# The first batch of an attention and maxout kernel: its transposes copied in two parts, and the order of its loads

## The chip, the cores and the metric

The kernel runs on one core of a Trainium2 chip. The metric is the device time of one execution in microseconds (us), as the median of several runs. The core has five engines that matter here, each working through its own instructions in order: TensorE (PE in the profile, with its weight loads shown as PEld), VectorE (DVE), ScalarE (ACT), GpSimd (POOL) and SyncE (SP). SP, ACT and POOL also issue DMA transfers; an issue stands in its engine's queue like any other instruction, and the transfer then runs on 16 DMA engines that all queues share.

## The reference

Attention over 8 batches, 12 heads, 448 tokens and 64 dimensions, with an extra term in the denominator, and behind it a feed-forward layer whose hidden value is the maximum of three products:

```python
scores = scale * np.matmul(q, k.transpose(0, 1, 3, 2))
m = np.max(scores, axis=-1, keepdims=True)
e = np.exp(scores - m)
attn = e / (np.sum(e, axis=-1, keepdims=True) + np.exp(-m) + 1e-09)
attn_out = np.matmul(attn, v)
...
x = attn_out.transpose(0, 2, 1, 3).reshape(B * S, H * D)   # 3584 x 768
h = np.maximum(np.maximum(x @ w1, x @ w2), x @ w3)
out = h @ w_out
```

All inputs and the output are float32; w1, w2, w3 and w_out are 768 x 768. With the maximum taken out, attn is exp(s) / (sum of exp(s) + 1), and this is what the kernel computes.

## The kernel before, in words

Two heads make a pair, p; a batch has NPAIR = 6 pairs, and there are NP = 48. One round `it` of the main loop computes the scores and exponentials of pair `it` and the weighted sums of pair `it - 1`.

*Loading.* `load` (L83) brings q, k or v of one or two pairs from DRAM with two DMAs each, since a tile has 128 partitions and 448 tokens are 7 chunks of 64. The upper DMA (L92) fills partitions 0 to 63 with chunks 0 to 3, the lower one (L93) partitions 64 to 127 with chunks 4 to 6. For one pair these are 128 KB and 96 KB. So a tile holds NB = 3 full chunks of 128 tokens and a last one of 64. The loads of batch 0 are issued on SP in the order in which they are written (L97 to L107), but for two halves of pair 0's that are issued on ACT. Tiles for raw data (`raw`, three sets of three pairs) are reused in turn.

*Casts.* `casts(p)` (L161) turns float32 into float16: `cast_qk` on DVE (L183 for q, L184 for k, L189 for k's last chunk, once for each head), and for pair 0 on ACT and DVE with the last chunk on POOL (L172 to L174, L189). `scale_v` (L191) multiplies v by 256 on POOL, in three instructions of line L157.

*Transposes.* `transposes(p)` (L204) makes PE transpose four chunks of q (L221) and four of k (L226) into one PSUM tile `trT`, 448 + 512 columns wide, and copies that to SBUF as `qkT`: for pair 0 in two parts (L230 on DVE, then L231 on ACT), for the others in one piece (L233 on DVE). From batch 2 on a DMA does the transposing.

*Scores.* `scores(p, c)` (L235) multiplies chunk c of k with all of q for both heads (L239), into one of two PSUM tiles; `exp_scores` (L249) takes the exponential on ACT. `scores_last` and `exp_last` (L255, L265) do the last chunk for both heads together.

*Sums.* In batch 0, `sums_main` and `sums_last` (L316, L325) give the denominators and the weighted sums apart, ACT takes the reciprocal as exp(-ln(x + 1)) (L336, L337), and DVE multiplies (L343). Later batches use L273, L285, L298, L299 and L307.

*Weights.* `load_weight` (L144) loads a matrix on POOL's queue, float32 to float16. The loop issues w1 in two halves in rounds 3 and 4 (L453), w2 in round 5, w3 in round 6 and w_out in round 8 (L455). In POOL's queue each stands behind the `scale_v` of the rounds before it.

*Feed-forward.* When a batch's attention is done, its groups are put into a queue (`batch_done`, L421): 18 groups of six matmuls (L356), six for each of w1, w2 and w3 in this order, then the output groups (L390). Rounds of the next batch take them from the queue one by one. The first three groups of batch 0, which need the first half of w1, are written out in rounds 5 and 6 (L482 to L508). The groups 3 to 5 of w1 follow in round 6, the first group of w2 is the first one of round 7.

*Filler.* `keep_busy(n)` (L345) issues n matmuls of zeros: 13 before pair 0's transposes, 3 behind them, 3 in each of the rounds 0 to 4 (L349).

The order of all instructions on each engine is the order in which the program writes them. A load on SP waits, besides for its tile, for the landing of the load eight places before it.

Of the kernel before, what the change touches and what calls it, by code (L numbers as in the profile page):

```python
# [21 lines left out]
def kernel(  # L22
# [57 lines left out]
        for i in range(NRAW)  # L80
    ]

    def load(p0, n_pairs, names="qkv", engs=(nc.sync, nc.sync)):  # L83
        b, j = divmod(p0, NPAIR)
        tiles = raw[(p0 // HB) % NRAW]
        h0 = 2 * (p0 % HB)
        for name, t, src in zip("qkv", tiles, (q, k, v)):
            if name not in names:
                continue
            rows = src[b, 2 * j : 2 * (j + n_pairs)].rearrange("h (p c) d -> p h c d", c=TP)  # L90
            hs = slice(h0, h0 + 2 * n_pairs)
            engs[0].dma_start(out=t[0:64, hs, 0 : NB + 1, :], in_=rows[:, :, 0 : NB + 1, :])  # L92
            engs[1].dma_start(out=t[64:128, hs, 0:NB, :], in_=rows[:, :, NB + 1 : TP, :])  # L93

    load(0, 1, "k", (nc.scalar, nc.sync))  # L97
    load(0, 1, "q", (nc.sync, nc.scalar))
    load(1, 1, "qk")
    load(0, 1, "v")  # L100
    load(2, 1, "qk")
    load(1, 2, "v")
    load(3, 1, "qk")
    load(4, 2, "q")
    load(3, 1, "v")
    load(4, 2, "k")
    load(4, 2, "v")  # L107

    idle = cpool.tile([128, S], MMDT, name="idle")
# [51 lines left out]
    def casts(p):  # L161
        cast_qk(p)
        scale_v(p)

    def cast_qk(p):
        qt, kt, _ = raw[(p // HB) % NRAW]
        h0 = 2 * (p % HB)
        hs = slice(h0, h0 + 2)
        k6, q6 = k16[p % NK], q16[p % NK]
        if p == 0:  # L170

            nc.scalar.copy(out=k6[:, 0:NB], in_=kt[:, hs, 0:NB].rearrange("p h c d -> p c h d"))  # L172
            for eng, cs in ((nc.scalar.copy, slice(0, 2)), (nc.vector.tensor_copy, slice(2, NB + 1))):
                eng(out=q6[:, cs], in_=qt[:, hs, cs].rearrange("p h c d -> p c h d"))  # L174
        else:
            if p >= P_DMA and (p // NPAIR) % 2:

                nc.vector.tensor_copy(
                    out=q6[:, 1 : NB + 1], in_=qt[:, hs, 0:NB].rearrange("p h c d -> p c h d")
                )  # L180
                nc.vector.tensor_copy(out=q6[64:128, 0], in_=qt[0:64, hs, NB])
            else:
                nc.vector.tensor_copy(out=q6, in_=qt[:, hs].rearrange("p h c d -> p c h d"))  # L183
            nc.vector.tensor_copy(  # L184
                out=k6[:, 0:NB], in_=kt[:, hs, 0:NB].rearrange("p h c d -> p c h d")
            )
        for hh, half in enumerate(halves):
            last = nc.gpsimd if p == 0 else nc.vector
            last.tensor_copy(out=k6[half, NB, hh], in_=kt[0:64, h0 + hh, NB])  # L189
# [14 lines left out]
    def transposes(p):  # L204
        odd = (p // NPAIR) % 2
        qkT = att_pool.tile([2 * D, 1024], MMDT, tag="qkT", bufs=3)
        qkTs[p] = qkT, 0, S
        if p >= P_DMA:
            nc.sync.dma_start_transpose(
                out=qkT.rearrange("q (c p) -> q c p", p=128),  # L210
                in_=qk16[p % NK].rearrange("p c h d -> p (c h d)"),
            )
            qkTs[p] = qkT, 64 * odd, 512
            return
        trT = ps_u.tile([128, 1024], MMDT, tag="u", name="trT")


        order = (NB, 0, 1, 2) if odd else (0, 1, 2, NB)
        n0 = 0
        for c in order:  # L220
            nc.tensor.transpose(  # L221
                out=trT[:, n0 : n0 + 128], in_=q16[p % NK][:, c], identity=ident16
            )
            n0 += SL if c == NB else 128
        for c in range(NB + 1):
            nc.tensor.transpose(  # L226
                out=trT[:, S + c * 128 : S + c * 128 + 128], in_=k16[p % NK][:, c], identity=ident16
            )
        if p == 0:
            nc.vector.tensor_copy(out=qkT[:, 0 : S + 128], in_=trT[:, 0 : S + 128])  # L230
            nc.scalar.copy(out=qkT[:, S + 128 : S + 512], in_=trT[:, S + 128 : S + 512])  # L231
        else:
            nc.vector.tensor_copy(out=qkT[:, 0 : S + 512], in_=trT[:, 0 : S + 512])  # L233

    def scores(p, c):  # L235
        qkT, q0, k0 = qkTs[p]
# [108 lines left out]
    def keep_busy(n):  # L345

        ps = ps_u.tile([128, 512], FP32, tag="u", name="busy")
        for _ in range(n):
            nc.tensor.matmul(out=ps[:, 0:S], lhsT=idle[:, 0:128], rhs=idle, start=True, stop=True)  # L349
# [81 lines left out]
            queue.pop(0)()  # L431

    LEFT = 4
    keep_busy(13)
    casts(0)
    transposes(0)
    keep_busy(3)
    for it in range(NP + 1):
        p = it if it < NP else None
        prev = it - 1 if it > 0 else None  # L440
# [14 lines left out]
            load_weight((5, 6, 8).index(it) + 1)  # L455
        if it < NPAIR:

            casts(it + 1)
            for c in range(2):
                exp_scores(p, c, scores(p, c))  # L460
            if prev is None:
                keep_busy(3)
                exp_scores(p, 2, scores(p, 2))
                transposes(1)
                exp_last(p, scores_last(p))
            else:
                den, av = (ps_av.tile([128, 512], FP32, tag="av", name=n) for n in ("den", "av"))
                sums_main(prev, den, 1)
                stp = scores(p, 2)
                sums_main(prev, av, 0)  # L470
                stl = scores_last(p)
                sums_last(prev, den, 1)
                sums_last(prev, av, 0)
                exp_scores(p, 2, stp)
                exp_last(p, stl)
                rb = reciprocals_one(den)
                transposes(it + 1)
            if it < NPAIR - 1:
                keep_busy(3)
            else:  # L480

                ups = [up_open()]  # L482
                up_part(ups[0], 0, 0, 0, range(3))
                av5 = ps_s.tile([128, 2, 512], FP32, tag="s", name="av5")
                sums_main(p, av5[:, 1], 1)
                sums_main(p, av5[:, 0], 0)
                sums_last(p, av5[:, 1], 1)
                sums_last(p, av5[:, 0], 0)
                rb5 = reciprocals_one(av5[:, 1])
            if prev is not None:  # L490
                normalize_one(prev, av, rb)
            if it == NPAIR - 1:
                normalize_one(p, av5[:, 0], rb5)
                batch_done(0)
        elif it == NPAIR:
            exp_scores(p, 0, scores(p, 0))

            up_part(ups[0], 0, 0, 0, (3,))
            ups.append(up_open())
            up_part(ups[1], 0, 0, 1, range(4))  # L500
            ups.append(up_open(ps_av, "av"))
            up_part(ups[2], 0, 0, 2, range(4))
            for dc in (4, 5):
                for fc, ps in enumerate(ups):
                    up_part(ps, 0, 0, fc, (dc,))
                    if dc == 5:
                        up_close(ps, 0, 0, fc)
            del queue[0:3]  # L508
            exp_scores(p, 1, scores(p, 1))
            group()  # L510
            casts(it + 1)
            exp_scores(p, 2, scores(p, 2))
            exp_last(p, scores_last(p))
            group()
            transposes(it + 1)
            group()
        else:
            late = it + 1 < P_DMA
            if not late:

                if it + 2 < NP:
                    cast_qk(it + 2)
                    transposes(it + 2)
                if it + 1 < NP:
                    scale_v(it + 1)
            if p is not None:
                for c in range(2):
                    exp_scores(p, c, scores(p, c))
            group()
            if late:  # L530
                casts(it + 1)
            avs = [av_main(prev, hh) for hh in range(2)]
            av_last(prev, avs)
            if p is not None:
                stp = scores(p, 2)
                stl = scores_last(p)
            rb = reciprocals(prev, avs)
            if p is not None:
                exp_scores(p, 2, stp)
                exp_last(p, stl)  # L540
            if late:
                transposes(it + 1)
            group()
            normalize(prev, 0, avs, rb)
            group()
            normalize(prev, 1, avs, rb)
            if it % NPAIR == 0:
                batch_done(prev // NPAIR)
            if it + 2 == P_DMA:
                cast_qk(it + 2)  # L550
                transposes(it + 2)
            for _ in range(n_groups - 3):
                group()
# [36 lines left out]
```

## Time and profile before

| What | Value |
|---|---|
| median of 3 runs | 368.15 us (368.03 to 368.56) |
| the profiled execution | 367.77 us |
| its span, first to last instruction | 366.0 us |
| granted TensorE clock, mean | 0.996 |
| scores of pair 0 start (PE, L239) | 7.08 us |
| scores of pair 1, 2, 3, 4, 5 start | 10.23, 14.53, 18.83, 23.48, 27.77 us |
| first matmul with w1 (PE, L356) | 31.16 us |
| DMA share of the 16 engines, 0 to 5 us and 20 to 25 us | 0.45 and 1.19 |

The profile's page begins with busy times: "busy" is time in which an engine's instructions run; issuing a DMA and waiting are not counted. In the list of groups, a row gives line, engine, operation, the tiles written and read, the shapes, the count, then the busy time in us and the mean of one in ns, and behind the second bar the idle time in front of these instructions, with what ended most of it. In the timeline a row is: start in us, duration in us, engine (with a "q" where its queue issues a DMA), line, operation, tiles, shapes, count, and in brackets the idle time before it and what ended it. Rows of one operation in a row are merged. The list of DMA issues ends with KB and us from issue to landing. In the list of DMA queues, q1 is SP's, q10 ACT's and q0 POOL's; its columns are packets, MB, and the time of the packets as a share of 16 engines. Shares can add up to a little over 100%, since packets overlap.

### The profile page before, as it was taken

What the parts mean: (1) busy time and instruction counts of PE and PEld (TensorE: products, weight loads), DVE (VectorE), ACT (ScalarE), POOL (GpSimd) and SP (SyncE); (2) the same over time, 40 slices, a digit from 0 to 9 for tenths busy, and PEclk for the clock granted to TensorE, in tenths of its full rate; (3) what the DMA queues carried; (4) which work ended last, traced back from release to release, by engine and by line L of the source; (5) the groups of instructions that cost most, each with busy time, mean ns of one, the idle gap of its engine ahead of it and who ended that gap; (6) DMA issues with size and microseconds to landing.
All of it is one profiled execution on the core that took longest, in us unless ns stands there. A gap on an engine that the chain in (4) does not pass through costs nothing.

```text
span 366.0 us, 6114 instructions
## 1 busy us (share of the span) xinstructions
PE 357.3 (98%) x2086; PEld 163.7 (45%) x2086; DVE 243.7 (67%) x521; ACT 220.6 (60%) x334; POOL 54.0 (15%) x159
## 2 busy tenths in 40 slices
PE   8999999999999999999999999999999999999994
PEld 3434444444444444444444444444444444445552
DVE  4564777876578677577657867757676876655553
ACT  4986476765666766666566676666566766651000
POOL 4263112211211211211121121121112112000000
PEclk9999999999999999999999999999999999999998
DMA  5999997668877879939764887847775673004006
GB/s 151 228 238 231 232 243 194 167 174 214 169 183 174 209 186 131 220 101 199 181 167 119 179 213 177 159 124 211 172 174 131 162 203 84 0 7 125 2 0 172
DMA packets 87792, 58.61 MB, mean 160 GB/s; under 512 B 43473, under 2 KB 84177, under 8 KB 87761
## 3 DMA queue, kind: packets, MB, share of 16 engines
q1 hardware_dynamic: 83552, 53.27, 60.7%
q0 software_dynamic: 3920, 4.72, 7.4%
q8 instruction: 16, 0.26, 0.3%
q10 hardware_dynamic: 288, 0.23, 0.2%
q14 instruction: 16, 0.12, 0.1%
HBM read 42.47 MB, written 11.01 MB: 146 GB/s over the span
## 4 chain that ended last, share of the span: by engine, by line
PE 94%; DVE 2%; ACT 1%; DMA 1%; issue 0%; SPq 0%; DVEq 0%
PE up L356 45%; PE op L390 15%; PE av L273 13%; PE stp L239 9%; PE stl L255 4%; PE av L285 3%; PE av L316 1%; DMA qin<-in_q_dram 1%; ACT eT L249 1%; PE trT L226 1%; PE trT L221 1%; DVE qkT L233 1%; DVE o_sb L400 0%; PE av L325 0%; PE busy L349 0%
## 5 line engine op out<-in xcount | busy, mean ns | idle before, releaser
L356 PE MATMUL up<-xT,w 128*128 128x448 f16 x864 | 175.3, 353 | 0.7 <-DVE xT L307 0.4
L249 ACT ACTIVATE eT<-stp 128x896 f16<-128x896 f32 x144 | 125.5, 910 | 53.9 <-PE stp L239 53.8
L356 PEld LDWEIGHTS <-w 128*128 128x128 f16 x864 | 81.6, 98 | 81.7 <-issue 12.5
L372 DVE TENSOR_TENSOR hT<-hT,up 128x448 f16<-128x448 f16 x96 | 59.6, 621 | 52.0 <-PE up L356 51.1
L157 POOL TENSOR_SCALAR vst<-vin 128x384 f16<-128x384 f32 x132 | 43.2, 338 | 255.1 <-issue 173.6
L298 ACT ACTIVATE lnd<-av 64x448 f32<-64x448 f32 x84 | 45.2, 538 | 48.9 <-PE av L285 47.9
L390 PE MATMUL op<-w,hT 128*128 128x384 f16 x336 | 59.3, 327 | 0.0
L273 PE MATMUL av<-eT,vst 128*128 128x448 f16 x252 | 54.5, 353 | 0.0
L307 DVE TENSOR_TENSOR xT<-av,rb 64x448 f16<-64x448 f32 x84 | 51.8, 617 | 1.4
L239 PE MATMUL stp<-qkT 64*128 64x448 f16 x288 | 44.1, 353 | 1.5 <-DVE qkT L233 0.7
L370 DVE CAST hT<-up 128x448 f16<-128x448 f32 x48 | 29.8, 624 | 22.9 <-PE up L356 22.2
L400 DVE TENSOR_SCALAR o_sb<-op 128x384 f32<-128x384 f32 x56 | 31.0, 553 | 20.0 <-PE op L390 19.0
L390 PEld LDWEIGHTS <-hT 128*128 128x128 f16 x336 | 31.6, 98 | 24.7 <-issue 4.0
L273 PEld LDWEIGHTS <-vst 128*128 128x128 f16 x252 | 24.6, 98 | 22.5
L184 DVE CAST qk<-kin 128x384 f16<-128x384 f32 x47 | 25.8, 549 | 1.8 <-DMA kin<-in_k_dram 1.4
L265 ACT ACTIVATE eL<-stl 128x448 f16<-128x448 f32 x48 | 25.9, 539 | 0.0
L299 ACT ACTIVATE rb<-lnd 128x448 f32<-128x448 f32 x42 | 24.2, 576 | 1.3
L239 PEld LDWEIGHTS <-qkT 64*128 64x128 f16 x288 | 11.0, 94 | 23.2 <-issue 16.8
L189 DVE CAST qk<-kin 64x64 f16<-64x64 f32 x94 | 17.9, 191 | 1.3
L255 PE MATMUL stl<-qkT 128*128 128x448 f16 x48 | 17.4, 363 | 0.0
L285 PE MATMUL av<-eL,vst 64*128 64x448 f16 x84 | 15.3, 360 | 0.0
L233 DVE COPY qkT<-trT 128x960 f16<-128x960 f16 x11 | 7.2, 656 | 9.9 <-PE trT L226 9.9
(49 smaller groups left out, 110.0 us busy)
## 6 DMA issues: line engine op xcount, KB each, us to landing
out_dram<-o_sb SPq DMA_DIRECT2D x56, 192.0 KB, 2.7
qin<-in_q_dram SPq DMA_DIRECT2D x46, 128.0 KB, 3.0
kin<-in_k_dram SPq DMA_DIRECT2D x45, 128.0 KB, 2.9
vin<-in_v_dram SPq DMA_DIRECT2D x44, 128.0 KB, 3.0
kin<-in_k_dram SPq DMA_DIRECT2D x46, 96.0 KB, 2.7
qin<-in_q_dram SPq DMA_DIRECT2D x45, 96.0 KB, 2.7
vin<-in_v_dram SPq DMA_DIRECT2D x44, 96.0 KB, 2.9
w<-in_moe_w_dram POOLq DMA_DIRECT2D x2, 1152.0 KB, 17.2
```

The lines of the kernel that those rows point to most:

```text
L157: nc.gpsimd.tensor_scalar(out=out, in0=in_, scalar1=LAMBDA, scalar2=1.0, op0=ALU.mult, op1=ALU.mult)
L239: nc.tensor.matmul(out=stp[:, hh, 0:S], lhsT=qkT[hh * D : hh * D + D, k0 + c * 128 : k0 + c * 128 + 128], rhs=qkT[hh * D : hh * D + D, q0 ...
L249: nc.scalar.activation(out=eT[:, p % 2, c], in_=stp[:, :, 0:S], func=AF.Exp, scale=scale)
L255: nc.tensor.matmul(out=stl[:, 0, 0:S], lhsT=qkT[:, k0 + NB * 128 : k0 + NB * 128 + 128], rhs=qkT[:, q0 : q0 + S], start=True, stop=True,)
L273: nc.tensor.matmul(out=av[:, 0:S], lhsT=vst[:, p % VB, hh * NB + c, (1 - hh) * D : (3 - hh) * D], rhs=eT[:, p % 2, c, hh, :], start=(c == ...
L298: nc.scalar.activation(out=lnd[mine], in_=avs[hh][other, 0:S], func=AF.Ln, bias=1.0)
L307: nc.vector.tensor_tensor(out=xTs[b][mine, j, :], in0=avs[hh][mine, 0:S], in1=rb[mine], op=ALU.mult)
L356: nc.tensor.matmul(out=ps[:, 0:S], lhsT=w_sb[i][:, dc, ts(fc, 128)], rhs=xTs[b][:, dc, :], start=(dc == 0), stop=(dc == NDC - 1),)
L370: nc.vector.tensor_copy(out=h, in_=ps[:, 0:S])
L372: nc.vector.tensor_tensor(out=h, in0=h, in1=ps[:, 0:S], op=ALU.max)
L390: nc.tensor.matmul(out=ps[:, 0:NW], lhsT=hTs[sb][:, fc, ts(t, 128)], rhs=wout_sb[:, fc, ts(nh, NW)], start=(fc == 0), stop=(fc == NFC - 1),)
L400: nc.vector.tensor_scalar(out=o_sb[:, ts(nh, NW)], in0=ps[:, 0:NW], scalar1=1.0 / LAMBDA, scalar2=None, op0=ALU.mult,)
```

## The change

Four things change, all in batch 0 and the first pair of batch 1.

1. *Pair 0's loads.* q comes first and k behind it, and k in two parts: its chunk 0 alone (with its counterpart in the lower partitions), then the rest. For this `load` gets a range of chunks. Upper halves are issued on SP, lower halves on ACT: three issues on each, where there were two.
2. *The order of later loads.* k of pairs 4 and 5 comes right behind their q, in front of v of pair 3.
3. *Transposes in two parts.* An inner function `rest(c0, c1)` transposes chunks c0 to c1 of k and copies what they add, on DVE. Pairs 1 to 6 copy q with the first chunk of k (576 columns), then the rest (384 columns). For pair 0 the second part is handed back to the caller, which calls it behind the scores and the exponential of chunk 0, and pair 1's casts come behind that. ACT no longer copies a part of pair 0's transposes.
4. *Filler and casts of pair 0.* 11 filler matmuls instead of 13 and 2 instead of 3. q is cast first, its halves on ACT and DVE; then chunk 0 of k on DVE and chunks 1 and 2 on ACT.

```diff
-    def load(p0, n_pairs, names="qkv", engs=(nc.sync, nc.sync)):
+    def load(p0, n_pairs, names="qkv", engs=(nc.sync, nc.sync), c0=0, c1=NB + 1):
...
-            engs[0].dma_start(out=t[0:64, hs, 0 : NB + 1, :], in_=rows[:, :, 0 : NB + 1, :])
-            engs[1].dma_start(out=t[64:128, hs, 0:NB, :], in_=rows[:, :, NB + 1 : TP, :])
-    load(0, 1, "k", (nc.scalar, nc.sync))
+            engs[0].dma_start(out=t[0:64, hs, c0:c1, :], in_=rows[:, :, c0:c1, :])
+            c2 = min(c1, NB)
+            engs[1].dma_start(
+                out=t[64:128, hs, c0:c2, :], in_=rows[:, :, NB + 1 + c0 : NB + 1 + c2, :]
+            )
     load(0, 1, "q", (nc.sync, nc.scalar))
+    load(0, 1, "k", (nc.sync, nc.scalar), 0, 1)
+    load(0, 1, "k", (nc.sync, nc.scalar), 1)
     load(1, 1, "qk")
     load(0, 1, "v")
     load(2, 1, "qk")
     load(1, 2, "v")
     load(3, 1, "qk")
-    load(4, 2, "q")
+    load(4, 2, "qk")
     load(3, 1, "v")
-    load(4, 2, "k")
     load(4, 2, "v")
...
-            nc.scalar.copy(out=k6[:, 0:NB], in_=kt[:, hs, 0:NB].rearrange("p h c d -> p c h d"))
             for eng, cs in ((nc.scalar.copy, slice(0, 2)), (nc.vector.tensor_copy, slice(2, NB + 1))):
                 eng(out=q6[:, cs], in_=qt[:, hs, cs].rearrange("p h c d -> p c h d"))
+            for eng, cs in ((nc.vector.tensor_copy, slice(0, 1)), (nc.scalar.copy, slice(1, NB))):
+                eng(out=k6[:, cs], in_=kt[:, hs, cs].rearrange("p h c d -> p c h d"))
...
-        for c in range(NB + 1):
-            nc.tensor.transpose(
-                out=trT[:, S + c * 128 : S + c * 128 + 128], in_=k16[p % NK][:, c], identity=ident16
-            )
+        def rest(c0, c1):
+            for c in range(c0, c1):
+                nc.tensor.transpose(
+                    out=trT[:, S + c * 128 : S + c * 128 + 128],
+                    in_=k16[p % NK][:, c],
+                    identity=ident16,
+                )
+            n0, n1 = (S + c * 128 if c else 0 for c in (c0, c1))
+            nc.vector.tensor_copy(out=qkT[:, n0:n1], in_=trT[:, n0:n1])
+
         if p == 0:
-            nc.vector.tensor_copy(out=qkT[:, 0 : S + 128], in_=trT[:, 0 : S + 128])
-            nc.scalar.copy(out=qkT[:, S + 128 : S + 512], in_=trT[:, S + 128 : S + 512])
+            rest(0, 1)
+            return rest
+        if p <= NPAIR:
+            rest(0, 1)
+            rest(1, NB + 1)
         else:
-            nc.vector.tensor_copy(out=qkT[:, 0 : S + 512], in_=trT[:, 0 : S + 512])
+            rest(0, NB + 1)
...
-    keep_busy(13)
+    keep_busy(11)
     casts(0)
-    transposes(0)
-    keep_busy(3)
+    k_rest = transposes(0)
+    keep_busy(2)
...
-            casts(it + 1)
+            if it > 0:
+                casts(it + 1)
             for c in range(2):
                 exp_scores(p, c, scores(p, c))
+                if it == 0 and c == 0:
+                    k_rest(1, NB + 1)
+                    casts(1)
```

## The prediction, made before the changed kernel ran

> **What bounds the kernel now.** I read the page first: busy time by engine, then the idle time in front of the costliest group.
>
> ```profile
> PE 357.3 (98%) x2086; PEld 163.7 (45%) x2086; DVE 243.7 (67%) x521; ACT 220.6 (60%) x334; POOL 54.0 (15%) x159
> ...
> L356 PE MATMUL up<-xT,w 128*128 128x448 f16 x864 | 175.3, 353 | 0.7 <-DVE xT L307 0.4
> ```
>
> TensorE (PE) is busy 98% of the span, and its largest group waited 0.7 us in all. Lost time after batch 0 is therefore not won back, and won time has to come from batch 0, where part of PE's work is filler (L349). There I read the timeline:
>
> ```profile
> 13.82 0.66 DVE L233 COPY qkT<-trT 128x960 f16<-128x960 f16 x1 [1.90 <-PE trT L226]
> ...
> 14.53 0.55 PE L239 MATMUL stp<-qkT 64*128 64x448 f16 x4 [0.18 <-DVE qkT L233]
> ...
> 14.94 2.54 ACT L249 ACTIVATE eT<-stp 128x896 f16<-128x896 f32 x3 [0.28 <-PE stp L239]
> ...
> 21.57 0.55 DVE L184 CAST qk<-kin 128x384 f16<-128x384 f32 x1 [0.82 <-DMA kin<-in_k_dram]
> ```
>
> A round lasts 4.30 us (scores at 10.23, 14.53, 18.83), ScalarE (ACT) idles 0.28 of it, and the copy L233 stands between transposes and scores. At 21.57 the cast of pair 4 waited 0.82 us for k; that round takes 4.65. Then GpSimd's (POOL's) timeline, and PE's where the second expert's weights are first used:
>
> ```profile
> 18.54 0.51 POOL L157 TENSOR_SCALAR vst<-vin 128x384 f16<-128x384 f32 x1 [2.24 <-DMA vin<-in_v_dram]
> 19.02 0.55 POOL L157 TENSOR_SCALAR vlast<-vin 64x64 f16<-64x64 f32 x2
> 19.52 1.01 POOL L147 DMA_DIRECT2D w<-in_moe_w_dram  x1
> ...
> 24.84 0.87 POOL L147 DMA_DIRECT2D w<-in_moe_w_dram  x1
> ...
> 26.76 0.87 POOL L147 DMA_DIRECT2D w<-in_moe_w_dram  x1
> ```
> ```profile
> 42.69 1.31 PE L356 MATMUL up<-xT,w 128*128 128x448 f16 x6
> ```
>
> POOL scales pair 3's v as soon as it lands (18.54) and only then issues the first half of w1's load (19.52). The second half follows at 24.84, w2's load at 26.76. The list of DMA issues, asked for one issue at a time, has the landings (last column, us from issue):
>
> ```profile
> w<-in_moe_w_dram POOLq DMA_DIRECT2D x1, 576.0 KB, 8.7
> ```
> ```profile
> w<-in_moe_w_dram POOLq DMA_DIRECT2D x1, 576.0 KB, 9.0
> ```
> ```profile
> w<-in_moe_w_dram POOLq DMA_DIRECT2D x1, 1152.0 KB, 14.8
> ```
>
> So the halves land at 28.2 and 33.8, and w2 at 26.76 + 14.8 = 41.6. Their first uses are at 31.16, 37.20 and, for w2, 42.69: slacks of 2.9, 3.4 and only **1.1 us**.
>
> **The change, part by part.** Sums are made on the profiled execution: span 366.0 and 1.77 around it, 367.77, which is 0.38 under the median of 368.15.
>
> *Loads of pair 0.* SP now has three issues (q, k chunk 0, rest of k) ahead of pair 1's q where it had two, ACT three instead of two; SP's issues stand 0.65 apart (13.54, 14.20, 14.86), so all later loads on SP leave 0.65 later. q, now first, lands when k did: 0.74 + 3.2 = 3.9 instead of 1.56 + 3.9 = 5.5. ACT's casts come after its issues in its queue; the third (about 2.2 to 2.9) ends before q lands, so nothing waits for it. The landing of chunk 0 (256-byte rows) is in no row: not before 1.56 + 2.8 = 4.4, the shortest landing there, not after 5.5, q's as second load. I take 4.8.
>
> *PE's start.* The 13 fillers run from 1.16 at 0.37 each until the clock rises; 11 end near 5.1. Before, eight transposes from 5.91 led to the copy at 6.57; five, at 0.06 each less, lead to it 0.48 after their start: 5.6 (chunk 0 at 4.8) to 6.0 (at 5.5, with 0.2 for its cast, near the 0.19 to 0.29 of the small DVE casts). The copy takes 0.46 (L230): scores at 6.1 to 6.5 instead of 7.08. But the second scores follow the first (0.38), three transposes (0.4 with their drain) and the copy of the rest, which moves from ACT to DVE: 384 columns, between 0.20 (what 384 more columns cost, 0.66 − 0.46) and ACT's 0.48, taken as 0.36. That is 7.3 to 7.6 against 7.59. Behind them come fillers and the third scores, in PE's order, and pair 1's casts (6.94 to 8.20 before), now queued behind the copy on DVE, end at 8.6 to 8.9, where PE transposes at 8.85. The 0.6 to 1.0 won shrinks to 0 to 0.3; I take 0.1.
>
> *The copy in two.* For pairs 2 to 5 the scores wait for L233 (0.18 each): with the first part they start 0.66 − 0.46 = 0.20 earlier, 0.8 over four rounds. The second part ends 0.46 + 0.36 + 0.03 = 0.85 after the first begins, the first scores at 0.46 + 0.05 + 0.38 = 0.89: hidden. DVE's next work, L343, waits for ACT anyway (14.69, 0.21 idle). Pair 1's copy lies beside 0.57 of filler, pair 6's beside `up` and sums: no gain.
>
> *k of pairs 4 and 5 ahead of v of pair 3.* Its lower half left at 16.16 and landed 5.3 later, 21.5. Now two issues earlier and 0.65 later, and behind 224 KB less (some 0.95 us at 234 GB/s, the rate from 10 to 21 us): 21.5 − 0.95 + 0.65 = 21.2; bounds 20.2 (if the shift is absorbed) and 21.5. The cast would be wanted at 20.2, so pair 4 gains 0.3 plus the split's 0.2, not 0.6; all pairs together bring batch 0's end forward by about 0.8 (0.7 to 1.4).
>
> *v of pair 3 behind them.* This price I take to decide. From 10 to 21 us the load queue is the bound:
>
> ```profile
> q1 hardware_dynamic: 3082, 2.56, 95.3%
> ```
>
> (packets, MB, share of the 16 engines.) v of pair 3 takes the place that k of pair 5 had: the same bytes in front, landing 21.5, plus the 0.65 of issue, 22.1. Bounds: 21.0 (shift absorbed, and a landing as prompt as v's before, 3.5 after issue) and 22.3. POOL needs 0.17 + 0.98 until it issues the weights: 23.25 instead of 19.52, **3.7 us later**. The attention has room: the scaled v is used near 24.5. The weights do not. Their queue (q0) in three windows, 22 to 26, 26 to 28 and 28 to 32 us:
>
> ```profile
> q0 software_dynamic: 737, 0.56, 93.2%
> ```
> ```profile
> q0 software_dynamic: 45, 0.03, 9.1%
> ```
> ```profile
> q0 software_dynamic: 758, 0.59, 95.3%
> ```
>
> Half one ran from 22.0, 2.4 after its issue, to 26 with stragglers to 28.2; the queue was then nearly empty for 2 us because half two had been issued late. That gap swallows part of the 3.7. Now half one starts at 23.25 + 2.4 = 25.65 and lasts 4.1 (its bulk) to 6.2 (its stragglers), taken as 4.5: the row without stragglers is nearer, since the load queue has 3 us to itself before. Half one is in at about 30.6, against 31.16 − 0.8: up to 0.3 of wait, no loss against before. Half two (issue about 25.4, POOL scaling pair 4 first) starts behind it at 30.15 instead of 28.05. Half two and w2 took 41.55 − 28.05 = 13.5 together. **w2 lands at 43.65**, bounds 42.6 (v at 21.0, short run) and 45.5.
>
> *Sum.* The first w2 matmul moves from 42.69 to 43.7, +1.0, whatever batch 0 has won, as PE stands there with the averages (L273), the later scores and casts behind it. Later weights have slack enough (29.78 + 19.6 = 49.4 for w3, used from 55.4). Span 366.0 + 1.0 = 367.0, execution 368.8; against the median, **369.15 us**. By the bounds of w2's landing: −0.1 to +2.8, 368.05 to 370.95.
>
> **Rivals.** (1) *The gains stand, faster.* v lands by 21.0 and the first half has no stragglers and packs into the empty 2 us, or half two's start stays at 28.05: w2 lands at 41.6 and batch 0's gain counts. It is at most the slack of 1.1; with 0.95 the execution takes 366.8, against the median 367.2. The point: w2's load must slip by less than 0.4. For it: the empty window 26 to 28. Against it: the window holds 2 us and the issue slips 3.7. (2) *Slip and slack nearly cancel.* The extra issue costs nothing, because the engines, 95% busy from 10 to 21 us, take up the 0.65: v lands at 21.5, POOL issues at 22.6, w2 lands at 43.0, and the execution takes 368.1, against the median 368.5. For it: that busy stretch. Against it: from 14 to 15 us the load queue moves only half of what it does beside it, so pair 4's q starts as soon as it is issued and carries the shift on. [...] (3) *It does not start earlier*: chunk 0 lands like a full load (5.5), and the scores come no earlier. That takes 0.1 to 0.3 from the gain, but under the main theory nothing from the time, 369.15; under (1) 367.4.
>
> [...]
>
> **How the numbers follow.** Main theory 0.6, faster 0.18, cancelling 0.22; rival 3 lies within these. About 0.2% (0.74 us) is what a measurement of this kernel can tell from no change. Of the main theory's landings I count a tenth as under +0.74, and of the cancelling case's a little over a quarter as beyond: slower 0.6, same 0.22, faster 0.18. The range leaves a tenth on each side: 367.2 to 370.2; the main theory's own is 368.4 to 370.4.
>
> **What would show it.** Right: v of pair 3 lands near 22, POOL issues the first weights near 23.2, PE idles 1 to 2.5 us before the first w2 matmul (seventh round) and that matmul starts after 42.7. Scores of pairs 2 to 5 start 0.05 after a 0.46 copy; the 0.82 wait shrinks. Wrong: the first weights issued before 22, or a w2 matmul before 42 without a wait. Another error would be DVE, with seven more copies, ending later than ACT in a round.

## The result and the profile after

| | Before | Changed |
|---|---|---|
| median of 4 runs each, one chip | 368.36 us (368.03 to 368.57) | **370.49 us** (370.11 to 370.72) |
| the profiled execution, its span | 367.77, 366.0 us | 370.72, 368.9 us |
| scores of pairs 0 to 5 start | 7.08, 10.23, 14.53, 18.83, 23.48, 27.77 | 6.66, 11.15, 15.90, 20.66, 25.41, 30.17 |
| first matmul with w1, with w2 | 31.16, 42.69 | 34.26, 45.80 |
| w2 lands | 41.53 | 44.44 |

The ratio is **1.0061** (1.0049 to 1.0073): slower, as forecast, but by 2.1 us where 0.8 over these runs' median (1.0 over the one of the prediction) was expected, and just outside the range. The profiles are 2.95 us apart in execution, more than the medians, because the profiled execution before took less than all four runs of its kernel in the table, and the changed one is the longest of its four.

The whole difference is made in batch 0. Pair 0 starts 0.42 earlier; pair 1 is 0.92 late; each of the next rounds takes 4.75 us where it took 4.30 (4.65 for the one in which pair 4's cast waited). In the table of waits from 5 to 35 us of the changed kernel, PE's rows are these (total us, times, longest):

```profile
PE trT L232 <- DVE qkT L238: 3.3, 6, 0.6
PE stp L254 <- DVE qkT L238: 0.5, 1, 0.5
```

The first row has no counterpart before: transposes that write `trT` wait for a copy that reads it, six times, 0.55 each. The changed kernel's timeline (start, duration) shows where that falls in a round; PE and DVE of pair 2:

```profile
14.09 0.39 PE L226 MATMUL trT<-ident,qk 128*128 128x128 f16 x4
14.31 0.22 PE L232 MATMUL trT<-ident,qk 128*128 128x128 f16 x1
...
15.08 0.33 PE L232 MATMUL trT<-ident,qk 128*128 128x128 f16 x3 [0.55 <-DVE qkT L238]
15.24 0.73 PE L364 MATMUL busy<-idle 128*128 128x448 f16 x3
15.90 0.55 PE L254 MATMUL stp<-qkT 64*128 64x448 f16 x4
```
```profile
14.57 0.46 DVE L238 COPY qkT<-trT 128x576 f16<-128x576 f16 x1 [1.23 <-PE trT L232]
...
15.44 0.36 DVE L238 COPY qkT<-trT 128x384 f16<-128x384 f16 x1 [0.42 <-PE trT L232]
```

The first copy runs from 14.57 to 15.03. PE stands until then, does the three transposes of chunks 1 to 3 at 15.08, then the three fillers behind them, and only at 15.90 the scores, 0.87 after the data they need was there. Of these 0.87 the fillers take 0.66 (15.24 to 15.90). Before, all eight transposes came first, the fillers lay beside the copy, and the scores followed it by 0.05. From the copy's start to the scores it is now 1.33 instead of 0.71; less 0.17 for the three transposes that used to stand ahead of the copy (0.06 each), that is the 0.45 of a round.

The weights are late too, as the prediction said. POOL's timeline in the changed kernel, and then PE's at the first w2 matmul:

```profile
22.69 0.51 POOL L161 TENSOR_SCALAR vst<-vin 128x384 f16<-128x384 f32 x1 [5.93 <-DMA vin<-in_v_dram]
23.16 0.55 POOL L161 TENSOR_SCALAR vlast<-vin 64x64 f16<-64x64 f32 x2
23.66 1.01 POOL L151 DMA_DIRECT2D w<-in_moe_w_dram  x1
...
25.73 0.87 POOL L151 DMA_DIRECT2D w<-in_moe_w_dram  x1
...
27.71 0.87 POOL L151 DMA_DIRECT2D w<-in_moe_w_dram  x1
```
```profile
45.31 0.55 PE L254 MATMUL stp<-qkT 64*128 64x448 f16 x4
45.80 1.31 PE L371 MATMUL up<-xT,w 128*128 128x448 f16 x6
```

The last of the three issues (27.71) is w2's. Its row in the list of DMA issues ends with 16.7 us to landing; it is in at 44.44:

```profile
w<-in_moe_w_dram POOLq DMA_DIRECT2D x1, 1152.0 KB, 16.7
```

The row of PE at 45.80 has no bracket: PE comes to w2 1.36 us after it is there. The late weights cost nothing here, because PE itself is 3.11 us late. The page's line of busy times hardly tells of the loss; for the changed kernel it is:

```profile
PE 357.7 (97%) x2083; PEld 164.2 (45%) x2083; DVE 244.1 (66%) x529; ACT 220.6 (60%) x333; POOL 53.9 (15%) x159
```

PE is as busy as before (357.3) over a span 2.9 longer. Its idle time went from 8.7 to 11.2 us (span less busy), and a share of 97% instead of 98% is all that the page makes of it; the waits above, 3.8 us in all, say where it is.

### The profile page after: what moved, and what is told of

The parts are those of the page before. It is cut to its first block, busy times and chain, and to the rows that moved or that the text cites. A ratio compares the mean times of both kernels' runs of the same rounds, so it can differ in the third digit from the quotient of the medians.

```text
span 368.9 us, 6119 instructions
## 1 busy us (share of the span) xinstructions
PE 357.7 (97%) x2083; PEld 164.2 (45%) x2083; DVE 244.1 (66%) x529; ACT 220.6 (60%) x333; POOL 53.9 (15%) x159
## 4 chain that ended last, share of the span: by engine, by line
PE 90%; DMA 4%; DVE 2%; ACT 1%; issue 1%; SPq 0%; DVEq 0%
PE up L371 44%; PE op L405 14%; PE av L288 13%; PE stp L254 8%; PE stl L270 3%; PE av L300 3%; DMA vin<-in_v_dram 2%; PE busy L364 2%; DMA kin<-in_k_dram 2%; ACT eT L264 1%; PE trT L232 1%; PE trT L226 1%; DVE qkT L238 1%; PE av L331 1%; DVE o_sb L415 0%
## 5 line engine op out<-in xcount | busy, mean ns | idle before, releaser
L238 DVE COPY qkT<-trT 128x576 f16<-128x576 f16 (+2 forms) x19 | 9.0, 473 | 15.1 <-PE trT L232 15.1
```

## The experiments

Four theories are told apart. **A**: the wait of the last transposes for the first copy, and the fillers behind it, make the loss. **B**, the prediction's: v of pair 3 lands late, so do the weights, and w2 sets the time. **C**: the new start of pair 0 has its own share in the loss. **D**, later: after a standstill of PE its clock is what costs. Times are medians in us, "before" being the unchanged kernel on the same chip in the same runs; the last two columns are of each one's profiled execution.

| Run | Median | Before | Ratio (95%) | First w2 matmul | w2 lands |
|---|---|---|---|---|---|
| e1_split_wait | 370.68 | 368.18 | 1.0069 (1.0056 to 1.0081) | 45.91 | 42.22 |
| e2_split_free | 367.59 | 368.18 | 0.9986 (0.9976 to 0.9997) | 42.54 | 41.98 |
| e3_loads_swapped | 368.64 | 368.18 | 1.0018 (1.0007 to 1.003) | 43.64 | 43.60 |
| e4_start_alone | 368.69 | 368.18 | 1.0012 (1.0004 to 1.0021) | 43.51 | 42.85 |
| e5_changed_free | 370.57 | 368.10 | 1.0067 (1.005 to 1.0085) | 44.50 | 44.45 |
| e6_changed_v_first | 370.57 | 368.10 | 1.0078 (1.0063 to 1.0093) | 45.61 | 42.97 |
| e7_v_on_pool | 369.23 | 368.10 | 1.0028 (1.0005 to 1.0051) | 43.96 | 41.33 |
| e8_v_on_pool_swapped | 368.77 | 368.10 | 1.0021 (1.0005 to 1.0037) | 42.54 | 41.18 |
| e9_best_old_start | **366.73** | 367.95 | **0.9965** (0.9951 to 0.9978) | 41.61 | 40.74 |
| e10_changed_free_v_first | 368.50 | 367.95 | 1.0013 (1.0004 to 1.0022) | 43.59 | 43.22 |
| e11_changed_free_again | 369.21 | 367.95 | 1.003 (1.0018 to 1.0043) | 44.92 | 44.87 |
| e12_changed_free_filled | 369.54 | 367.95 | 1.0039 (1.0025 to 1.0053) | 44.53 | 44.49 |

### The split alone, with and without the wait

e1_split_wait is the kernel before with the copies of pairs 1 to 6 in two as in the change, and nothing else:

```diff
-        for c in range(NB + 1):
+        split = 1 <= p <= NPAIR
+        for c in range(1 if split else NB + 1):
             ...
+        if split:
+            nc.vector.tensor_copy(out=qkT[:, 0 : S + 128], in_=trT[:, 0 : S + 128])
+            for c in range(1, NB + 1):
+                nc.tensor.transpose(
+                    out=trT[:, S + c * 128 : S + c * 128 + 128], in_=k16[p % NK][:, c], identity=ident16
+                )
+            nc.vector.tensor_copy(out=qkT[:, S + 128 : S + 512], in_=trT[:, S + 128 : S + 512])
```

> The kernel before with one part of the change alone: for pairs 1 to 6 the transposes of k's chunks 1 to 3 come behind the first copy, and a second copy follows. Theory A (the loss comes from those three transposes waiting for the copy of the same PSUM tile): each of these pairs costs 0.46 (copy) + 0.05 more between its transposes and its scores, of which the rounds before had 0.36 idle but the filler now comes later; the profile of the changed kernel shows rounds of 4.75 us for 4.30. So +0.45 for pairs 2 to 5, about +0.5 each for pair 1 and pair 6: first matmul with w1 near 34.0 instead of 31.16, time +2.3 to +2.9 us, 370.6 to 371.2. Theory B (late weights are the loss): nothing here delays them, the time stays within 0.3 of 368.3 or falls.

e2_split_free is the kernel before, where the two copies come behind all eight transposes:

```diff
+        elif p <= NPAIR:
+            for n0, n1 in ((0, S + 128), (S + 128, S + 512)):
+                nc.vector.tensor_copy(out=qkT[:, n0:n1], in_=trT[:, n0:n1])
```

> The kernel before with the copy of pairs 1 to 6 in two parts, but both behind all eight transposes, so that no transpose waits for a copy. Theory A: the scores of pairs 2 to 5 start 0.2 us earlier each (a copy of 0.46 instead of 0.66 in front of them), rounds of 4.10, first matmul with w1 near 30.4, time -0.7 to -0.9 us, 367.5, as long as w2 (landing near 41.6) does not stop PE. Rival (ScalarE or the second copy takes the place of the first wait): rounds stay at 4.25 to 4.30 and the time within 0.2 of before.

e1 alone loses 2.5 us, no less than the whole change. Its waits from 5 to 35 us have one row for PE:

```profile
PE trT L233 <- DVE qkT L231: 3.3, 6, 0.5
```

Its w2 lands at 42.22, early, and is first used at 45.91: A, without any of B. e2 has the same two copies and gains 0.14%. In its timeline:

```profile
13.15 0.39 PE L226 MATMUL trT<-ident,qk 128*128 128x128 f16 x4
```
```profile
13.57 0.72 DVE L234 COPY qkT<-trT 128x576 f16<-128x576 f16 x2 [1.73 <-PE trT L226]
...
21.83 0.55 DVE L184 CAST qk<-kin 128x384 f16<-128x384 f32 x1 [1.81 <-DMA kin<-in_k_dram]
```
```profile
14.09 0.63 PE L242 MATMUL stp<-qkT 64*128 64x448 f16 x4
```

The row of 0.72 merges both copies (x2); scores start 0.52 after the first begins. Rounds 1 and 2 take 4.10 (9.99, 14.09, 18.19), the 0.20 less that the prediction had for them. Round 3 takes 5.35, because pair 4's cast now waits 1.81 for k, where it waited 0.82; so 0.6 us are left in the end, under the 0.7 to 0.9 expected.

### The loads alone

e3_loads_swapped is the kernel before with the new order of the loads:

```diff
-    load(4, 2, "q")
+    load(4, 2, "qk")
     load(3, 1, "v")
-    load(4, 2, "k")
```

> The kernel before with k of pairs 4 and 5 loaded in front of v of pair 3, nothing else. Theory B (what the prediction said of the weights): v of pair 3 lands near 21.4 instead of 18.4, the first half of w1 is issued near 22.6, w2 lands near 43.0 (42.6 to 43.6) and stops PE in round 7; batch 0 gains the 0.35 us that the cast of pair 4 waited, and loses it again: +0.2 to +0.9 us. Theory A alone (only the copies matter, weights have room): -0.35 us, 368.0.

```profile
22.52 1.01 POOL L146 DMA_DIRECT2D w<-in_moe_w_dram  x1
```
```profile
41.72 0.55 PE L238 MATMUL stp<-qkT 64*128 64x448 f16 x4
43.64 1.31 PE L355 MATMUL up<-xT,w 128*128 128x448 f16 x6 [1.37 <-DMA w<-in_moe_w_dram]
```

This is POOL's and PE's timeline of e3, and it is theory B to the row: the weights leave 3.0 later than before (22.52, was 19.52), batch 0 runs 0.5 ahead (first w1 matmul 30.67), and PE stands 1.37 for w2, which lands at 43.60. So B is real and costs 0.46 us net (368.64 against 368.18) when PE is on time.

### The new start

e4_start_alone is the changed kernel with one copy for pairs 1 to 6 and the old place of pair 3's v:

```diff
-        if p <= NPAIR:
-
-            rest(0, 1)
-            rest(1, NB + 1)
-        else:
-            rest(0, NB + 1)
+        rest(0, NB + 1)
...
-    load(4, 2, "qk")
+    load(4, 2, "q")
     load(3, 1, "v")
+    load(4, 2, "k")
```

> The changed kernel's start alone: pair 0's q first and k in two loads, 11 and 2 fillers, pair 0's transposes in two parts with pair 1's casts behind them; one copy for pairs 1 to 6, and v of pair 3 in its old place. In the changed kernel the first scores came 0.42 us earlier and the second and third 0.28 later. Theory C (the start costs what pair 0's second scores lose): pair 1's scores 0.2 to 0.4 later, time +0.2 to +0.4. Theory A alone: the same scores come within 0.1 of 10.23, time unchanged. If the loads, 0.65 later on SP, matter, pair 4's cast waits 1.4 instead of 0.82 and the time is +0.7 to +1.0.

```profile
22.39 0.55 DVE L190 CAST qk<-kin 128x384 f16<-128x384 f32 x1 [2.45 <-DMA kin<-in_k_dram]
```

The start itself gains: scores at 5.76, pair 1 at 9.72 (0.5 before the old kernel), pair 3 at 18.32. Then pair 4's cast waits 2.45, in e4's timeline of DVE above, and its scores come at 24.30, 0.8 late. That k lands at 22.27, 0.8 later than before, and is issued 0.66 later (16.82, was 16.16): one issue more stands ahead of it on SP. The kernel loses 0.5 us; C holds for the loads that the start pushes back, not for the start. The wait is longer than the 1.4 expected, since DVE comes to it earlier.

### Mending the changed kernel

e5_changed_free is the changed kernel with all transposes ahead of the two copies; e6_changed_v_first is the changed kernel with pair 3's v in its old place (the second part of e4's diff); e10_changed_free_v_first has both. The edit of e5:

```diff
-        if p <= NPAIR:
-
-            rest(0, 1)
-            rest(1, NB + 1)
-        else:
-            rest(0, NB + 1)
+        for c in range(NB + 1):
+            nc.tensor.transpose(
+                out=trT[:, S + c * 128 : S + c * 128 + 128],
+                in_=k16[p % NK][:, c],
+                identity=ident16,
+            )
+        for n0, n1 in ((0, S + 128), (S + 128, S + 512)) if p <= NPAIR else ((0, S + 512),):
+            nc.vector.tensor_copy(out=qkT[:, n0:n1], in_=trT[:, n0:n1])
```

> The changed kernel with the two copies of pairs 1 to 6 behind all eight transposes, so that no transpose waits for a copy; loads, fillers and pair 0 as changed. Theory A+B (the copies' waits hide a second limit, the late weights): PE would reach w2 near 42, and stands there until w2 lands, near 44.4 as in the changed kernel; the time is only 1.0 to 1.6 us under the changed kernel, 369.0 to 369.5, still 0.9 to 1.4 over before. Theory A alone: all of the loss goes, and the gains of start and split show: 367.0 to 367.6.

> The changed kernel with v of pair 3 in its old place, in front of k of pairs 4 and 5; the split copies with their waits stay. Theory A+B: the weights land about 1.5 us earlier, but PE, late by the copies' waits, does not wait for them: no change, 370.2 to 370.8, unless pair 4's cast waits for k, and PE is too late for that too. Theory B alone (the order of v is the loss): back to 368.5 or below.

> The changed kernel with both mended: copies in two parts behind all transposes, v of pair 3 in its old place. Theory A+B: the weights land near 42.9 as in the run of the start alone, pair 4's cast waits for k as there (scores near 24.2), PE reaches w2 near 43.1, a little after it landed: time 367.9 to 368.5, that is 2 us under the changed kernel, where each mend alone gave nothing. Theory A alone (order of v without effect): the same time as with the copies mended alone.

e6 lands w2 at 42.97 and uses it at 45.61: with the waits of the split still there, earlier weights change nothing (370.57). e5 takes the waits away, and B comes out from behind them; its timeline of PE:

```profile
42.18 0.55 PE L256 MATMUL stp<-qkT 64*128 64x448 f16 x4
...
44.50 1.31 PE L373 MATMUL up<-xT,w 128*128 128x448 f16 x6 [1.76 <-DMA w<-in_moe_w_dram]
```

PE is ready at 42.74 and stands 1.76. This execution took 369.4, but the three others of e5 took 370.47 to 370.79, no better than the changed kernel. So the same kernel ran again on another chip, as e11_changed_free_again, and beside it e12_changed_free_filled, for theory D: e12 puts six fillers in front of the first w2 group, so that PE doesn't stand still there.

```diff
+            if it == NPAIR + 1:
+                keep_busy(6)
             group()
```

> The changed kernel with the copies mended alone, once more, beside the other two of this call: its profile had w2's first matmul at 44.50 and 369.4 us in the execution profiled, but 370.5 to 370.8 in the three others. Theory B: w2's landing stops PE for over 1.5 us in every execution; w2's first matmul at 44.3 to 45.6, 369.2 to 370.8. If it is faster than 368.5, the weights were late by chance.

> As the run beside it (copies mended, v behind k), with six filler matmuls (1.1 us) in front of the first w2 group of round 7, where PE stands still for about 1.8 us. Theory D (some executions lose a further 1.2 us because TensorE's clock falls after the standstill, as it fell to half from 8.4 to 11.9 us in the first version with v on POOL's queue): the time falls to 369.1 to 369.6 in all executions. Rival (the spread comes from the landing of w2): no difference, or up to 0.3 slower.

e11 took 369.21, with the same wait for w2 (first w2 matmul 44.92, w2 in at 44.87), 1.3 us over the kernel before and, by the two ratios, 0.3% under the changed one. e12 took 369.54, with intervals that overlap: filling the standstill changes nothing here. But no execution of e11 took over 369.9, so the further loss that D is to explain didn't come up in these two runs, and they can't decide on D. In the one execution of e5 that has a trace the granted clock stayed at 1.00 through the standstill. The three that took over 370.4 have none; their mean granted clocks are 0.994, 0.995 and 0.997, where the traced one has 0.997, so a lower clock is on record for two of the three alone, and why they took longer stays open. With pair 3's v moved back as well, e10 is down to 368.50, still 0.13% over the kernel before: w2 lands at 43.22 and is used at 43.59. What remains is the wait of pair 4's scores (24.57) for k, which lands at 22.74.

### A version that beats both

What the rows ask for: two copies without the wait, k of pair 4 earlier, the weights no later. SP issues a load every 0.65 us (13.54, 14.20 and 14.86 in the kernel before), so taking loads off SP should bring those behind them forward. e7_v_on_pool is e10 with v of pairs 0 to 2 issued on POOL's queue and all the rest of pair 0's k on ACT's; e8_v_on_pool_swapped has the changed order of pair 4's k and pair 3's v besides. e7's edit, from e10:

```diff
-    load(0, 1, "k", (nc.sync, nc.scalar), 1)
+    load(0, 1, "k", (nc.scalar, nc.scalar), 1)
     load(1, 1, "qk")
-    load(0, 1, "v")
     load(2, 1, "qk")
-    load(1, 2, "v")
...
     make_identity(nc, ident16)
+    load(0, 1, "v", (nc.gpsimd, nc.gpsimd))
...
-    casts(0)
+    cast_qk(0)
+    load(1, 2, "v", (nc.gpsimd, nc.gpsimd))
+    scale_v(0)
```

> A version meant to beat both: copies of pairs 1 to 6 in two parts behind all transposes, the changed start with the rest of pair 0's k issued on ACT only, v of pairs 0 to 2 loaded from POOL's queue so that SP has four issues fewer, v of pair 3 in its old place. If the order and pace of issues on SP set the landings (theory B): all later loads leave up to 2.6 us earlier, pair 4's cast does not wait, weights leave earlier, w2 does not stop PE: rounds of 4.1, w2's first matmul near 41.2, time 366.5 to 367.2. Rival (the DMA engines are the limit and packets of POOL's queue push the others back): 367.6 to 368.5.

> As the version with v on POOL's queue, but with k of pairs 4 and 5 in front of v of pair 3. Theory B: v of pair 3 lands 1.5 to 2.5 us later than in the other, the first weights are issued that much later, and w2 stops PE if it lands after 41.2: 367.2 to 368.5, slower than the other by 0.3 to 1.5. Rival (with SP's issues freed the order of these two does not matter): within 0.2 of the other.

Both missed. Pair 0's second scores come at 8.69 and 8.65 (7.59 before), since the rest of its k, now all issued on ACT, lands and is cast later (in e7 the last of it lands at 7.41, against 5.20 in the changed kernel, and the transposes wait 0.77 for ACT's cast). From there on both traces run rounds of 4.10 without a wait for k or w2, but from a late start. Besides, six of e7's ten executions and five of e8's took 1 to 3 us longer than the others, at a lower granted clock (see the last section), and the medians are drawn up by these.

e9_best_old_start therefore keeps the start and the order of the kernel before, with e2's edit, and moves only the v loads, behind POOL's two casts of pair 0:

```diff
     load(1, 1, "qk")
-    load(0, 1, "v")
     load(2, 1, "qk")
-    load(1, 2, "v")
     load(3, 1, "qk")
...
     keep_busy(13)
-    casts(0)
+    cast_qk(0)
+    load(0, 1, "v", (nc.gpsimd, nc.gpsimd))
+    load(1, 2, "v", (nc.gpsimd, nc.gpsimd))
+    scale_v(0)
```

> The kernel before with two things: the copies of pairs 1 to 6 in two parts behind all transposes, and v of pairs 0, 1 and 2 loaded from POOL's queue (behind its two copies for pair 0), four issues of SP fewer. The start is that of before. If SP's pace of issues set pair 4's wait and the weights' landing: pair 1's scores at 10.0, rounds of 4.10 without a wait at pair 4, w2 landed by 41.3 (41.2 and 41.3 in the two versions with v on POOL's queue), its first matmul near 41.4: 366.6 to 367.1. Rival (POOL's packets push the first loads of SP back, or a wait for v of pair 0 comes up): 367.4 to 368.3.

e9's timelines of DVE, POOL and PE:

```profile
20.23 0.55 DVE L182 CAST qk<-kin 128x384 f16<-128x384 f32 x1
...
22.08 0.72 DVE L232 COPY qkT<-trT 128x576 f16<-128x576 f16 x2 [0.99 <-PE trT L224]
```
```profile
17.46 0.89 POOL L145 DMA_DIRECT2D w<-in_moe_w_dram  x1
```
```profile
41.61 1.31 PE L357 MATMUL up<-xT,w 128*128 128x448 f16 x6
```

Pair 4's cast no longer waits (no bracket at 20.23), so that all rounds take 4.1 (10.30, 14.39, 18.50, 22.59, 26.70). The first weights leave 2.1 earlier than before, w2 lands at 40.74, and PE takes it at 41.61 without waiting. The median is 366.73, within the 366.6 to 367.1 expected, **0.35% below** the kernel before and, by the two ratios (0.9965 and 1.0061), about 1% below the changed kernel.

## Why the prediction was wrong

**The step that failed is "the copy in two".** It set the end of the second part (0.85 after the first begins) against the end of the first scores (0.89) and called it hidden. That counts DVE's work alone. Between the two copies stand PE's transposes of chunks 1 to 3, and they write the tile that the first copy is reading. In the changed kernel the second part ended 1.23 after the first began (14.57, 15.80), not 0.85, and the first scores only began at 1.33. The step asked who waits for the copy and not what the copy makes wait. Nor did it look at what PE has queued behind those transposes: fillers that had been cover for the copy and now stand ahead of the scores. Instead of 0.20 earlier, each round came 0.45 later (4.75, 4.30); against a split without the wait (4.10) the wait costs 0.65 a round. Pairs 1 and 6, whose old copy lay wholly beside other work, lose 0.7 each where "no gain" was put: pair 1 starts at 11.15 here and at 10.48 in e5, which has the same start but not the wait, and w1 follows pair 5's scores by 4.09 us instead of 3.39. The 0.20 itself was right: e2 has it. How much of the 0.65 is the wait's and how much the fillers' no run tells apart. By the rows of pair 2, fillers ahead of the three transposes would lie in the wait of 0.55, and a round would take some 4.1 (4.75 less 0.66, an estimate). Pair 6 has no filler there and loses 0.7 all the same.

Why the three transposes wait: in the trace it is the copy that ends their wait (six times, 3.3 us in all), though they write other columns of `trT`. The first write starts 0.05 after the copy's end (15.03, 15.08), and as much after it in e1 (14.91, 14.96). Whether the copy and these writes could overlap is not shown, since no run lets them. A second tile for chunks 1 to 3 was not tried.

**The v and weights steps were right in kind, and hidden.** v of pair 3 landed at 22.52 (forecast 22.1, just over the bounds of 21.0 to 22.3), the first weights left at 23.66 (23.25), half one was in at 31.24 (30.6) and w2 at 44.44 (43.65, bounds 42.6 to 45.5). "+1.0, whatever batch 0 has won" was the weak sentence: it allowed for a batch 0 that wins less, not for one that loses 3. Where PE is on time the wait is there, as forecast: 1.37 in e3, 1.76 in e5, 1.73 in e11. e3's first w2 matmul at 43.64 is close to the forecast's 43.7, but e3 lacks the extra issue on SP; with the changed start and loads w2 landed at 44.45 and 44.87 (e5, e11), 0.8 to 1.2 later than forecast. That the change came out slower, as forecast, was luck as far as the cause goes: the late w2 that was to make it slower cost nothing in the changed kernel. An idle PE before the first w2 matmul was named as the sign of the theory, and it was absent in the changed kernel; scores 0.05 after a 0.46 copy were absent too.

**k of pairs 4 and 5.** Its halves landed at 19.57 and 20.33; the lower one was forecast at 21.2 (bounds 20.2 to 21.5). Pair 4's cast stopped waiting: right in kind. In e3 this brings pair 4's scores 0.5 forward. The gain is not safe, though. In e5, e12 and e11, which load in the changed order and whose rounds take 4.10, the lower half landed at 21.32, 21.71 and 22.28, although it was issued at 15.51 in all three as in the changed kernel, and pair 4's cast waited 0.95, 1.29 and 2.56 for k. Why the landing differs by 2 us between executions stays open.

**The start.** q landed at 3.83 and chunk 0 at 4.37 (3.9, 4.8). First scores at 6.66, second at 7.87, third at 8.84: 0.3 behind the old ones from the second on, not 0.1 before them. In e4 they came at 5.76, 6.85 and 7.82, the later two 0.7 before the old ones. The term goes with the time of the rise of PE's clock (6.95 in the changed kernel, 4.27 in e4), which is told below. That all later loads on SP leave 0.65 later was right: in e4 they did, and there it cost 0.8 at pair 4.

**Why the parts don't add up.** Alone, the split loses 2.5, the loads 0.46 and the start 0.5; the change as a whole loses 2.1. The waits of the split make PE late enough that neither the weights nor k of pair 4 is late for it any more. Rivals 1 and 2 assumed that batch 0 gains, and are out for the same reason as the main theory's sum; rival 3 (no earlier start) holds in this profile from the second scores on and decided nothing.

## What to carry to other kernels

When a copy is cut so that the reader may start sooner, follow the tile in both directions. Here the writes left between the two parts waited for the first one, 0.55 us each time, and everything queued behind them waited too: rounds took 4.75. With all writes ahead of both parts they took 4.10 (e2, rounds 1 and 2). The filler that had covered the copy covered nothing once it stood behind that wait, and took 0.66 more, so look at what else is in the queue between a wait and the work that matters. And a delay that one change makes can hide another's: the order of the loads cost 0.46 alone (e3), and mending it in the changed kernel gained nothing (370.57, e6) while the split's waits stood. So mend and measure parts alone before they are put down as harmless.

## What was unexpected of the hardware

PE's clock did not rise at a fixed time. All 14 profiles start matmuls at 1.15 or 1.16 us, and the trace's record of full clock begins between 4.27 (e4) and 7.20 us (e12); before had 4.87, the changed kernel 6.95. Fillers start 0.37 apart until then and 0.19 after (4.49, 4.87, 5.06 and 5.25 in the kernel before), so by their pace the clock was half of full before. (The views print 1.00 for that time, too, since nothing is on record for it.) With the new start, the later the rise, the later pair 1 begins: 9.72, 9.83, 10.29, 10.48 and 10.52 for rises at 4.27, 5.10, 6.54, 7.01 and 7.20 (e4, e11, e10, e5, e12). The 14 rises are spread over 2.9 us; what sets the time of the rise is not shown.

In e7 the clock fell again. Its windows by time (us, then busy time of PE, PEld, DVE, ACT and POOL, granted clock, DMA share, GB/s):

```profile
5.10:8.40 3.30, 1.97 (x13) 0.66 (x12) 1.13 (x4) 1.04 (x3) 2.45 (x7) 1.00 0.69 152
8.40:11.80 3.40, 3.11 (x16) 1.40 (x17) 1.30 (x5) 1.97 (x3) 0.58 (x2) 0.51 1.03 246
```

After 3.3 us in which PE was busy for 1.97, it ran 3.4 us at half clock (third number from the right), and pair 1's scores came at 12.64 where e8, with its transposes as late (7.86 and 7.89) but its clock kept, had 11.23. So a like gap went with 1.4 us more in the one execution than in the other. That PE's idle time made the clock fall is not shown: in e5 PE was busy for 1.66 us from 41.14 to 44.56, a smaller share, and the clock stayed at 1.00.

The times of e7 and e8 go with the mean granted clock of each execution:

| Mean granted clock | e7, us | e8, us |
|---|---|---|
| 0.998 to 1.000 | 367.63 to 368.11 (4 executions) | 367.72 to 368.24 (5) |
| 0.995 | 369.12 to 369.62 (3) | 369.30 to 369.82 (5) |
| 0.987, 0.988 | 370.53 to 370.79 (3) | none |

Only one execution of each has a trace, e7's of the middle group (369.12) and e8's of the first (367.72). Where the clock was kept, both took about as long as the kernel before (368.10) in spite of their late start.
